# Two tiles per tanh in the last layer group of a fused attention and MLP kernel, with new scheduler priorities

## The chip, the cores and the metric

The kernel runs on one core of a Trainium2 chip. The metric is the device time of one execution in microseconds (us), the median of several runs. The profile is of one such execution.

## The reference

A sketched polynomial attention gives each of 4 x 1088 tokens a vector of 128 numbers (4 heads of 32), and an MLP without bias follows. Cut to what is computed:

```python
def phi(x):                       # S1, S2: 8 x 32
    a = einsum('rd,bhsd->bhsr', S1, x); b = einsum('rd,bhsd->bhsr', S2, x)
    return einsum('bhsi,bhsj->bhsij', a, b).reshape(..., 64)
kv = einsum('bhsf,bhsd->bhfd', phi(k), v);  z = sum(phi(k), axis=2)
x = einsum('bhsf,bhfd->bhsd', phi(q), kv) / (einsum('bhsf,bhf->bhs', phi(q), z)[..., None] + 1e-06)
x = x.transpose(0, 2, 1, 3).reshape(4352, 128)
h = x @ w_in                      # 128 x 2048
out = (h - tanh(h)) @ w_out       # 2048 x 128
```

q and k are drawn with a deviation of 0.5, v with 0.1. Inputs and the output are float32.

## The kernel before

The linear part h @ w_out is x @ (w_in @ w_out); the product of the two weights is formed once on the chip, as a high and a low bf16 part (`whi`, `wlo`). What is left is minus tanh(h) @ w_out, so the scalar engine (ACT) computes tanh with a scale of -1.

Two kinds of groups run over the tokens. Nine attention groups (`GROUPS`) of up to 20 blocks of 32 tokens go through these steps: `qT` transposes q, `p` projects it (L717, tiled f32 matmuls), `qq`, `au`, `dn`, `rd`, `an`, `qp` and `qpT` form products and denominators on the vector engine and GpSimd, `w` computes the numerators (L733, tiled f32 matmuls), and `x` casts the result to bf16 into `xT` (L812). The keys of each batch are handled by `kp` (L608, tiled f32 matmuls), `wk`, `gram`, `sums`, `turn`.

Eleven layer groups (`LAYERS` = 8, 14, 12, 14, 14, 14, 14, 12, 14, 12, 8 blocks of 32 tokens) do the MLP. In group g, for each of the 16 blocks jb of 128 hidden units:

- `h{g}_{jb}` (L898): one matmul of a 128 x 128 block of `w_in` with the group's tokens, into one of three PSUM banks that take turns (`h_bank`, banks 4 to 6);
- `t{g}_{jb}` (L902): one tanh on ACT from that bank into slot (16 g + jb) mod 40 of `tt`;
- `y{g}_{jb}` (L912): one matmul of a block of `w_out` with that slot, adding up in bank 7.

In group 0 (256 tokens) two blocks share a bank and a tanh (`two` is 2). The last two groups (9 with 384 tokens, 10 with 256) go through `last_rows`: tokens are the output's rows, so each `y{g}_{jb}_{y}` (L933) is a matmul of 128 tokens of a slot with a block of `w_out`, into a bank of its own for each 128 tokens y. `l{g}_{y}whi` and `l{g}_{y}wlo` add the linear part. Then a copy to SBUF (L942) and a store (L944) for each y; the last store is issued from ACT's queue.

The order of the work isn't written out. Every operation is put down with its engine, a cost, its dependencies and a priority (`P.op`). `Program.listed` plans in simulated time: it takes the engine that can start first, and of its operations that can start within 20 ns of that the one with the smallest priority number. On the tensor engine it prefers operations of the same kind (`mode`) as the last, and charges `MODE` = 92 ns for a change of kind. The planned order of each engine is then issued in order, with semaphores. An h or a t has priority 16 g + jb, a y that plus `LAG` = 12 (in `last_rows`, plus 10 + 0.1 y for group 9 and plus 12 + 8 y for group 10), and attention steps the priority of the layer group that needs them, less a few. `SHIFT` is a table of numbers added to the priorities of named operations:

```python
for tag, by in SHIFT.items():
    P.tags[tag].prio += by
```

The lines that the change touches are the table and these two at the head of the loop over hidden blocks:

```python
two = 1 if g else 2
for jb in range(0, NJB, two):
```

Of the kernel before, what the change touches and what calls it, by code (L numbers as in the profile page):

```python
# [15 lines left out]
NJB = DFF // 128  # L16
# [29 lines left out]
class Program:  # L46
# [210 lines left out]
    def emit(self):  # L257
# [64 lines left out]

SHIFT = {
# [21 lines left out]
}  # L345
TURNED = (0, 1, 3)

# [1 line left out]
def bass_polysketch_attn__then__act_tanh_shrink_kernel(nc, q, k, v, S1, S2, moe_w_in, moe_w_out, out):  # L349
    P = Program(nc)  # L350
# [4 lines left out]
    def pe(n):  # L355
        return n / 2.4 + 2.7

    def dve(n):
        return 100 + n / 0.96

    def act(n):
        return 52 + n / 1.2
# [53 lines left out]
    def h_bank():  # L416
        i = 4 + (n_hb[0] + 2) % NHB
        n_hb[0] += 1
        return ps[:, i, :], bank[i]
# [31 lines left out]
    NL = len(lays)  # L451
# [419 lines left out]
    def store(g):  # L871
        ob = out.rearrange("(b j c) e -> b j c e", b=B, j=32)
        o, u = 0, g % 2
        for b, c, nb in lays[g][0]:
            for cb in range(4):
                P.op("sync", 4096 * nb / 250, lambda e, b=b, c=c, nb=nb, cb=cb, o=o: e.dma_start(
                    out=ob[b, :, c:c + nb, 32 * cb:32 * cb + 32],
                    in_=osb[u][32 * cb:32 * cb + 32, 32 * o:32 * (o + nb)].rearrange("p (c x) -> p c x", x=32)),
                    r=[("osb", u)], sem=f"out{u}", prio=NJB * g)
            o += nb  # L880

    def layers(g):
        parts, nb, t0, of = lays[g]
        n = 32 * nb
        slot0 = NJB * g

        def lin(front):
            for x, nm in ((whi, "whi"), (wlo, "wlo")):
                P.op("tensor", pe(n), lambda e, x=x, f=front and x is whi, l=not front and x is wlo: e.matmul(  # L889
                    acc[:, 0:n], x[:, :], xT[:, t0:t0 + n], start=f, stop=l),  # L890
                    r=[(nm,)] + [("xT", x) for x in of], w=[ka], prio=slot0 + LAG + (0 if front else NJB))

        two = 1 if g else 2
        for jb in range(0, NJB, two):
            s = slot0 + jb
            bk, kb = h_bank()
            ts = s % TSLOTS
            P.op("tensor", two * pe(n), lambda e, jb=jb, bk=bk: [e.matmul(  # L898
                bk[:, n * x:n * x + n], w_in[:, 128 * (jb + x):128 * (jb + x) + 128], xT[:, t0:t0 + n], start=True, stop=True)
                for x in range(two)][-1],  # L900
                r=[("w_in", jb // 4)] + [("xT", x) for x in of], w=[kb], prio=s, tag=f"h{g}_{jb}")
            P.op("scalar", act(n * two), lambda e, ts=ts, bk=bk: e.activation(  # L902
                out=tt[:, ts:ts + two, 0:n], in_=bk[:, 0:n * two].rearrange("p (x n) -> p x n", x=two), func=AF.Tanh, scale=-1.0),
                r=[kb], w=[("t", ts + x) for x in range(two)], prio=s, tag=f"t{g}_{jb}")
        if g >= NL - ROWS:
            return last_rows(g)
        if g > 1:
            lin(True)
        for jb in range(NJB):
            s = slot0 + jb  # L910
            ts = s % TSLOTS
            P.op("tensor", pe(n), lambda e, jb=jb, ts=ts: e.matmul(  # L912
                acc[:, 0:n], w_out[:, jb, :], tt[:, ts, 0:n],
                start=(jb == 0 and g < 2), stop=(jb == NJB - 1 and g != 1)),
                r=[("w_out", jb // 4), ("t", ts)], w=[ka], prio=s + LAG, tag=f"y{g}_{jb}")
        if g == 1:
            lin(False)
        u = g % 2
        ob, ok = (osb[u], ("osb", u)) if g else (osx, ("osx",))
        P.op("vector", dve(n), lambda e: e.transpose(out=ob[:, 0:n], in_=acc[:, 0:n]),  # L920
             r=[ka], w=[ok], prio=slot0, tag=f"o{g}")
        if g:
            store(g)

    def last_rows(g):
        ((b, c, nb),), _, t0, of = lays[g]
        slot0 = NJB * g
        last = g == NL - 1
        o, banks, eng = (0, (2, 3), ("sync", "scalar")) if last else (2, (7, 0, 1), ("sync",) * 3)
        ob = out.rearrange("(b j c) e -> b j c e", b=B, j=32)  # L930
        for y in range(nb // 4):
            def rows(lhs, rhs, prio, r, first=False, last=False, y=y, tag=None):
                P.op("tensor", 56, lambda e: e.matmul(  # L933
                    ps[:, banks[y], 0:128], lhs, rhs, start=first, stop=last), r=r, w=[bank[banks[y]]], prio=prio, tag=tag)

            for x, nm in ((whi, "whi"), (wlo, "wlo")):
                rows(xT[:, t0 + 128 * y:t0 + 128 * y + 128], x[:, :], slot0 + (LAG if last else 10), [(nm,)] + [("xT", x) for x in of], nm == "whi", tag=f"l{g}_{y}" + nm)
            for jb in range(NJB):
                ts = (slot0 + jb) % TSLOTS
                rows(tt[:, ts, 128 * y:128 * y + 128], w_out[:, jb, :], slot0 + jb + (LAG + 8 * y if last else 10 + 0.1 * y),  # L940
                     [("w_out", jb // 4), ("t", ts)], False, jb == NJB - 1, tag=f"y{g}_{jb}_{y}")
            P.op("vector", dve(128), lambda e, y=y: e.tensor_copy(osl[:, o + y, :], ps[:, banks[y], 0:128]),  # L942
                 r=[bank[banks[y]]], w=[("osl", o + y)], prio=slot0, tag=f"o{g}_{y}")
            P.op(eng[y], 300, lambda e, y=y: e.dma_start(  # L944
                out=ob[b, :, c + 4 * y:c + 4 * y + 4, :], in_=osl[:, o + y, :]),
                r=[("osl", o + y)], sem=f"outl{o + y}", prio=slot0, mode="rows")
# [27 lines left out]
    for g in range(NG):  # L974
# [18 lines left out]
        if g == 1:  # L993
            layers(0)
        if g == 2:
            linear_turn(1, DUE_W - 3)
            linear_product(DUE_W)
            first_linear(DUE_W + 4)
            layers(1)
# [65 lines left out]
```

## Time and profile before

| | us |
|---|---|
| median of three runs | 102.39 (102.28 to 102.39) |
| the profiled execution | 102.28 |
| its span, from the first to the last profiled instruction | 100.5 |

| engine | busy us | instructions |
|---|---|---|
| PE, matmuls | 96.5 | 1231 |
| PEld, weight loads | 52.0 | 1231 |
| DVE, vector engine | 71.5 | 181 |
| ACT, scalar engine | 78.0 | 182 |
| POOL, GpSimd | 33.2 | 60 |

PE is the tensor engine's matmuls, PEld its weight loads, which overlap them. Matmuls are pipelined and their ends are modelled, so that a matmul's duration is longer than the time from its start to the next one's; the starts are what counts. In a group's line, the number after "|" is the busy time, then the mean ns of one, then the idle time before them and what ended it. In a line of the timeline or the chain the first number is the start, the second the duration in us, and "x4" says that four neighbours were merged. In the windows the columns are busy time and count of each engine, the granted clock, the share of the DMA engines and GB/s. L898 is line 898 of the kernel before.

### The profile page before, as it was taken

How to read it: one execution, taken by the hardware profiler on the slowest of the kernel's cores; microseconds unless marked ns; L12 is line 12 of the kernel's file. 1: busy time of each engine (PE TensorE's matmuls, PEld its weight loads, DVE VectorE, ACT ScalarE, POOL GpSimd, SP SyncE). 2: the span in 40 equal slices, each digit the busy share in tenths (PEclk: the TensorE clock that was granted, in tenths of full speed). 3: DMA queues.
4: the chain of work that ended last, by engine and by line, in shares of the span. 5: the costliest groups of instructions: out<-in, count | busy, mean ns of one | idle time of the engine just before them, and what ended most of it. 6: DMA issues, size and time to landing. Idle time of an engine off the chain costs nothing.

```text
span 100.5 us, 3032 instructions
## 1 busy us (share of the span) xinstructions
PE 96.5 (96%) x1231; PEld 52.0 (52%) x1231; DVE 71.5 (71%) x181; ACT 78.0 (78%) x182; POOL 33.2 (33%) x60
## 2 busy tenths in 40 slices
PE   6999999999999999999999999999999999999980
PEld 5446467544666444545544444455444444468970
DVE  3689977999869999978999999899577226002140
ACT  0005679998957849793899998898999999999960
POOL 5577388042842400596040029403018000000000
PEclk9999999999999999999999999999999999999998
DMA  2899978920389451310899032002201403100512
GB/s 77 284 281 236 382 237 290 325 66 4 71 285 231 121 91 26 52 33 0 258 273 231 5 49 42 7 0 39 45 14 22 69 0 60 25 0 12 98 42 75
DMA packets 22510, 11.21 MB, mean 112 GB/s; under 512 B 16096, under 2 KB 21216, under 8 KB 22496
## 3 DMA queue, kind: packets, MB, share of 16 engines
q1 hardware_dynamic: 18976, 7.44, 30.5%
q10 hardware_dynamic: 3520, 3.57, 11.5%
q8 instruction: 9, 0.15, 0.6%
q14 instruction: 5, 0.04, 0.1%
HBM read 8.78 MB, written 2.23 MB: 110 GB/s over the span
## 4 chain that ended last, share of the span: by engine, by line
PE 87%; DMA 5%; DVE 4%; ACT 2%; issue 1%; POOL 0%; POOLq 0%; DVEq 0%
PE ps L898 31%; PE ps L912 24%; PE ps L733 5%; PE ps L933 5%; PE ps L673 5%; PE ps L717 4%; PE ps L608 3%; PE ps L889 3%; DMA kraw<-in_k_dram 3%; ACT tt L902 2%; DMA out_dram<-osl 2%; DVE wk L634 1%; PE ps L547 1%; PE ps L849 1%; PE ps L645 1%; PE ps L684 1%
## 5 line engine op out<-in xcount | busy, mean ns | idle before, releaser
L902 ACT ACTIVATE tt<-ps 128x448 bf16<-128x448 f32 (+3 forms) x168 | 71.9, 544 | 6.5 <-PE ps L898 6.0
L898 PE MATMUL ps<-xT,w_in 128*128 128x448 bf16 (+2 forms) x176 | 50.7, 333 | 0.2
L912 PE MATMUL ps<-tt,w_out 128*128 128x448 bf16 (+2 forms) x144 | 39.3, 338 | 0.0
L898 PEld LDWEIGHTS ps<-xT,w_in 128*128 128x128 bf16 x176 | 16.2, 98 | 20.4 <-ACT tt L902 11.5
L634 POOL TENSOR_TENSOR wk<-kab 128x256 f32<-128x256 f32 (+1 forms) x18 | 12.2, 675 | 19.1 <-DVE kab L619 17.5
L792 POOL TENSOR_TENSOR qp<-an,qq 128x512 f32<-128x512 f32 (+5 forms) x12 | 12.4, 1033 | 18.4 <-DVE an L780 17.5
L912 PEld LDWEIGHTS ps<-tt,w_out 128*128 128x128 bf16 x144 | 14.1, 98 | 7.7 <-issue 0.5
L920 DVE STREAM_TRANSPOSE osb<-ps 128x448 f32<-128x448 f32 (+1 forms) x8 | 5.0, 627 | 11.4 <-PE ps L912 11.4
L799 DVE STREAM_TRANSPOSE qpT<-qp 128x448 f32<-128x448 f32 (+5 forms) x18 | 11.4, 658 | 0.3 <-POOL qp L792 0.2
L933 PE MATMUL ps<-w_out,tt 128*128 128x128 bf16 x80 | 8.1, 219 | 0.0
L681 ACT ACT_TABLE_LOAD x1 | 1.3, 1283 | 8.3 <-issue 8.3
L1035 POOL MEMSET mark<- 128x1 f32 x1 | 0.1, 99 | 22.3 <-DMA out_dram<-osl 22.3
L746 DVE STREAM_TRANSPOSE qq<-ps 128x448 f32<-128x448 f32 (+5 forms) x9 | 6.0, 671 | 1.7 <-PE ps L717 1.5
L547 PE MATMUL ps<-const-bfloat16-1.0 128*128 128x256 bf16 (+1 forms) x25 | 6.5, 394 | 0.8 <-PEq L1050 0.8
L812 DVE CAST xT<-ps 128x448 bf16<-128x448 f32 (+4 forms) x8 | 6.2, 773 | 1.5 <-PE ps L733 1.4
L933 PEld LDWEIGHTS ps<-w_out,tt 128*128 128x128 bf16 x80 | 6.4, 98 | 0.6
L601 DVE STREAM_TRANSPOSE kT<-kraw 128x576 f32<-128x576 f32 (+1 forms) x8 | 5.7, 730 | 1.0 <-DMA kraw<-in_k_dram 0.9
L695 DVE STREAM_TRANSPOSE qT<-qraw 128x448 f32<-128x448 f32 (+5 forms) x9 | 5.9, 654 | 0.2 <-DMA qraw<-in_q_dram 0.2
L733 PE MATMUL ps<-qpT,ndw 64*32 64x288 f32 (+5 forms) x144 | 5.7, 373 | 0.0
L717 PE MATMUL ps<-qT,wq 64*32 64x288 f32 (+5 forms) x144 | 5.7, 373 | 0.0
L634 DVE TENSOR_TENSOR wk<-kab,ps 128x512 f32<-128x512 f32 x8 | 5.4, 673 | 0.0
L673 PEld LDWEIGHTS ps<-wk,vx 128*32 128x32 f32 x288 | 4.3, 110 | 1.8 <-issue 1.6
(86 smaller groups left out, 89.0 us busy)
## 6 DMA issues: line engine op xcount, KB each, us to landing
kraw<-in_k_dram SPq DMA_DIRECT2D x3, 544.0 KB, 4.1
qraw<-in_q_dram SPq DMA_DIRECT2D x3, 544.0 KB, 6.0
vx<-in_v_dram SPq DMA_DIRECT2D x10, 144.0 KB, 4.2
out_dram<-osb SPq DMA_DIRECT2D x20, 56.0 KB, 1.9
w_in_f<-in_moe_w_in_dram ACTq DMA_DIRECT2D x2, 512.0 KB, 8.1
w_out_f<-in_moe_w_out_dram ACTq DMA_DIRECT2D x2, 512.0 KB, 8.9
vx<-in_v_dram SPq DMA_DIRECT2D x4, 112.0 KB, 5.6
out_dram<-osb SPq DMA_DIRECT2D x8, 48.0 KB, 1.9
```

Of the source, the lines that this page charges most:

```text
L547: P.op("tensor", 213 if x < 12 else 290, lambda e, n=1 if x < 16 else 2: e.matmul(ps[:, 3, 0:256 * n], ones[:, 0:128], ones[:, None, :].to ...
L634: P.op(eng, 60 + 64 * n if eng == "vector" else pool(64 * n), lambda e: e.tensor_tensor(out=wk[:, t0:t1, :, :].rearrange("p t h (i j) -> p ...
L673: ins = e.matmul(ps[32 * h:32 * h + 32, sbk, 0:64], vx[i][:, h, t, :], wk[:, t, h, :], start=(t == 0), stop=(t == 8), tile_position=(0, 32 ...
L717: ins = e.matmul(o, wq[64 * r:64 * r + 64, b, y, :, :].rearrange("p h x -> p (h x)"), src, start=True, stop=True, tile_position=(64 * r, 3 ...
L733: ins = e.matmul(ps[32 * h:32 * h + 32, 2 + u, 0:32 * nh], ndw[i][64 * u:64 * u + 64, 32 * h:32 * h + 32], src[64 * u:64 * u + 64, h // 2, ...
L792: P.op("vector" if dv else "gpsimd", 95 + 33.2 * m if dv else pool(32 * m), lambda e, lo=lo, dv=dv: e.tensor_tensor(out=qp[u][:, lo:lo + m ...
L799: P.op("vector", dve(32 * m), lambda e, lo=lo: e.transpose(out=qpT[u][:, 32 * lo:32 * (lo + m)], in_=qp[u][:, lo:lo + m, :].rearrange("p n ...
L812: P.op("scalar" if early else "vector", (act if early else dve)(32 * nb) - 35, lambda e: (e.copy if early else e.tensor_copy)(xT[:, x0:x0 ...
L898: P.op("tensor", two * pe(n), lambda e, jb=jb, bk=bk: [e.matmul(bk[:, n * x:n * x + n], w_in[:, 128 * (jb + x):128 * (jb + x) + 128], xT[: ...
L902: P.op("scalar", act(n * two), lambda e, ts=ts, bk=bk: e.activation(out=tt[:, ts:ts + two, 0:n], in_=bk[:, 0:n * two].rearrange("p (x n) - ...
L912: P.op("tensor", pe(n), lambda e, jb=jb, ts=ts: e.matmul(acc[:, 0:n], w_out[:, jb, :], tt[:, ts, 0:n], start=(jb == 0 and g < 2), stop=(jb ...
L933: P.op("tensor", 56, lambda e: e.matmul(ps[:, banks[y], 0:128], lhs, rhs, start=first, stop=last), r=r, w=[bank[banks[y]]], prio=prio, tag ...
```

## The change

The number of blocks per tanh becomes a list: 2 for all of group 0 as before, seven times 2 and then 1 and 1 for the last group, 1 elsewhere. The names `h10_1`, `h10_3` and so on up to `h10_13` no longer exist (a pair has its first block's name), and likewise for t. In `SHIFT` 3 entries go (`h10_5`, `h10_7`, `h10_13`), 23 get another number and 43 are new. The loop, and those entries that the text speaks of:

```diff
-        two = 1 if g else 2
-        for jb in range(0, NJB, two):
+        jb = 0
+        for two in [2] * 8 if g == 0 else [2] * 7 + [1, 1] if g == NL - 1 else [1] * NJB:
             s = slot0 + jb
             bk, kb = h_bank()
             ts = s % TSLOTS
-            P.op("tensor", two * pe(n), lambda e, jb=jb, bk=bk: [e.matmul(
+            P.op("tensor", two * pe(n), lambda e, jb=jb, bk=bk, two=two: [e.matmul(
...
-            P.op("scalar", act(n * two), lambda e, ts=ts, bk=bk: e.activation(
+            P.op("scalar", act(n * two), lambda e, ts=ts, bk=bk, two=two: e.activation(
...
+            jb += two
         if g >= NL - ROWS:
             return last_rows(g)
```

```
name      before   after
y1_9        15.0    26.1
turn2       92.7    54.2
p8           5.8    59.8
w8         128.0    77.7461
h10_5       -5.4       -
h10_7      -28.6       -
h10_13     -11.8       -
h5_14          -    34.2
w3             -   -34.1
kp2            -   267.2
h9_0           -    17.0
h10_6          -   -45.5
...
```

The other new numbers are of the same kinds: most belong to h and y operations of groups 1 to 10, a few to steps of the keys and of the attention groups.

44 rows, old and new, of the table SHIFT are left out of this document.

## The prediction

> **What bounds the kernel now.** I began with the page: the engine totals, the chain, and the costly groups.
>
> ```profile
> PE 96.5 (96%) x1231; PEld 52.0 (52%) x1231; DVE 71.5 (71%) x181; ACT 78.0 (78%) x182; POOL 33.2 (33%) x60
> ...
> PE 87%; DMA 5%; DVE 4%; ACT 2%; issue 1%; POOL 0%; POOLq 0%; DVEq 0%
> ...
> L902 ACT ACTIVATE tt<-ps 128x448 bf16<-128x448 f32 (+3 forms) x168 | 71.9, 544 | 6.5 <-PE ps L898 6.0
> ```
>
> The chain that ended last is matmuls for 87% of the span and ACT for 2%. TensorE's busy time is modelled, so 96% alone proves nothing; the chain and the start times must. ACT's 168 tanhs were kept idle 6.0 us by matmuls. So ACT is a second, nearly full engine behind TensorE. The change edits ACT's work in the last layer group (group 10, 256 tokens wide) and the order of work everywhere, so I asked which engine sets the pace in the last 15 us: the windows that part the span where group 10's first hidden matmul starts (92.08), and the chain from 82 us on.
>
> ```profile
> core 0: us, PE busy (x) PEld busy (x) DVE busy (x) ACT busy (x) POOL busy (x), PEclk, DMA share, GB/s
> 92.08:97.54 5.46, 5.46 (x82) 5.03 (x78) 0.88 (x4) 5.13 (x18) 0.00 (x0) 1.00 0.35 67
> 85.00:92.08 7.08, 7.08 (x60) 4.37 (x60) 0.65 (x1) 7.08 (x19) 0.00 (x0) 1.00 0.09 15
> ```
> ```profile
> by line: PE ps L898 41.5%; PE ps L933 31.2%; PE ps L912 20.4%; PE ps L733 4.5%; PE ps L889 2.4%; DVE osl L942 1.9%; issue 0.2%
> ...
> 84.78 0.19 PE ps L898
> 84.96 0.19 PE ps L912
> ...
> 92.36 0.28 PE ps L933 x5
> ...
> 96.72 0.80 PE ps L933 x14
> 97.54 0.29 DVE osl L942
> ```
>
> Both engines look full in both windows. The chain decides: from 82 us on it holds no ACT piece at all. Matmuls follow each other without a gap (448 columns at 84.78, the next at 84.96), the 128-column rows of L933 at 0.28 / 5 = 0.056 us each. After the last row come a copy and the output store. ACT is hidden behind TensorE, if barely.
>
> How much TensorE still loses in the last stretch I worked out by counting, from the windows of L933 and of L898 alone and from the timeline:
>
> ```profile
> 92.08:97.54 5.46, 5.46 (x66) 4.81 (x62) 1.00 0.35 67
> ```
> ```profile
> 92.08:97.54 5.46, 4.38 (x16) 1.52 (x16) 1.00 0.35 67
> ```
> ```profile
> 91.86 0.39 PE L933 MATMUL ps<-w_out,tt 128*128 128x128 bf16 x4
> ...
> 92.08 0.27 PE L898 MATMUL ps<-xT,w_in 128*128 128x256 bf16 x1
> ...
> 93.40 0.27 PE L898 MATMUL ps<-xT,w_in 128*128 128x256 bf16 x1
> ...
> 93.51 0.28 PE L933 MATMUL ps<-w_out,tt 128*128 128x128 bf16 x2
> ```
>
> Of the 66 rows of L933 four had started before 92.08 (the row at 91.86), so 62 are issued in the stretch, and 16 hidden matmuls. A hidden matmul holds the issue for 93.51 - 93.40 = 0.11 us. So 62 x 0.056 + 16 x 0.11 = 3.47 + 1.76 = 5.23 us of issue. The stretch runs from 92.08 to 96.72 + 0.80 = 97.52, which is 5.44 us. TensorE idles 5.44 - 5.23 = 0.21 us there, and no more.
>
> **The change part by part.**
>
> **The paired tanhs.** The change removes seven of group 10's sixteen tanhs: 14 tiles of 256 columns go into seven instructions of 512, the last two stay single. It removes no matmul: each pair's two hidden matmuls write the two halves of one bank. What ACT saves comes from two rows, the single form in the lines of the last stretch, and four queued tanhs of the 512 form (group 0's, already paired) in ACT's timeline:
>
> ```profile
> L902 ACT ACTIVATE tt<-ps 128x256 bf16<-128x256 f32 x16 | 4.6, 456 | 0.0
> ```
> ```profile
> 13.55 2.07 ACT L902 ACTIVATE tt<-ps 128x512 bf16<-128x512 f32 x4 [0.48 <-PE ps L898]
> ```
>
> Successive instructions overlap, so I take the pitch and not the duration. Singles: (4.6 - 0.456) / 15 = 0.276 us. Pairs: with the four lasting about 0.62 each, (2.07 - 0.62) / 3 = 0.483 us. A pair saves at most 2 x 0.276 - 0.483 = 0.069 us, seven save 0.48 us of ACT. But TensorE's work per tile, one hidden matmul and three rows, is 0.11 + 3 x 0.056 = 0.278 us, the same as the singles' pitch: TensorE can give ACT nothing faster. So the saving reaches the end only as far as it removes TensorE's idle 0.21 us. Bounds: 0 and 0.21. I take 0.2, because with two tiles per bank three banks hold six tiles rather than three, and a hidden matmul that waits for a bank is the only wait that I see in that stretch.
>
> The Trainium skill (ScalarE: Activation LUTs, What ACT_TABLE_LOAD costs) gives an ACTIVATE with immediates 186 ns + 0.833 N and an overlap of 93 ns, an estimated fixed 0.093 us per instruction, or 0.65 us for seven; the rows give 0.48, and neither gets past TensorE.
>
> **What the pairing adds.** A row that reads the first tile of a pair now waits for the longer tanh, 0.62 instead of 0.456 us, and for the second hidden matmul (0.11): 0.27 us later. What covers it is the rows left from group 9: of the 62, 32 belong to group 10 and 4 are its linear terms, so 26 are group 9's, worth 26 x 0.056 = 1.46 us. Cost nothing; without that cover 0.27 us once. The last two tiles stay single, so the end after the last tanh is as it was: rows, copies, stores. The last store starts from ACT's queue behind the tanhs, but waits for the last copy, so a shorter ACT does not bring it forward.
>
> **The priorities.** 66 operations get a new one. No instruction is added or removed; TensorE's order changes. What an order can win is where TensorE loses time now. Apart from the 0.21 us I see one repeated loss: a run of tiled f32 matmuls (L608, L717, L733, 16 instructions each) stops the issue before and after it. Two of these in a row pay once. From TensorE's timeline, two alone and a joined couple:
>
> ```profile
> 62.45 0.36 PE L898 MATMUL ps<-xT,w_in 128*128 128x448 bf16 x1
> 62.75 0.66 PE L733 MATMUL ps<-qpT,ndw 64*32 64x256 f32 x16
> 63.20 0.58 PE L717 MATMUL ps<-qT,wq 64*32 64x224 f32 x16
> 63.72 0.36 PE L898 MATMUL ps<-xT,w_in 128*128 128x448 bf16 x1
> ```
> ```profile
> 75.62 0.55 PE L898 MATMUL ps<-xT,w_in 128*128 128x384 bf16 x2
> 76.10 0.61 PE L733 MATMUL ps<-qpT,ndw 64*32 64x224 f32 x16
> 76.64 0.50 PE L898 MATMUL ps<-xT,w_in 128*128 128x384 bf16 x2
> ...
> 82.10 0.36 PE L898 MATMUL ps<-xT,w_in 128*128 128x448 bf16 x1
> 82.39 0.77 PE L733 MATMUL ps<-qpT,ndw 64*32 64x320 f32 x16
> 83.09 0.36 PE L898 MATMUL ps<-xT,w_in 128*128 128x448 bf16 x1
> ```
>
> Alone, 224 columns hold the issue 76.64 - 76.10 = 0.54 us and 320 columns 0.70, so 256 would hold it about 0.59 (a third of the way). Joined, 256 columns held it 0.45 and the following 224 columns 0.52. That saves 0.14 + 0.02. The second also doesn't pay the lead-in again: the hidden matmul at 82.10 held the issue 0.29 us instead of 0.19, so 0.10. A join is worth about 0.26 us. The planner charges 92 ns (MODE, line 27) for it, a third, so an order that it thinks better can break a join, or make one by the way. There are four such joins now, in the chain:
>
> ```profile
> 16.93 0.54 PE ps L733 x16
> 17.47 0.33 PE ps L717 x16
> ...
> 23.73 0.65 PE ps L608 x16
> 24.38 0.32 PE ps L733 x16
> ...
> 44.89 0.65 PE ps L717 x16
> 45.54 0.43 PE ps L733 x16
> ...
> 62.82 0.59 PE ps L733 x16
> 63.41 0.38 PE ps L717 x16
> ```
>
> The new shifts reach several runs that stand alone: w3 (-34.1) and kp2 (+267.2), turn2 (92.7 to 54.2) between p6 and w5, and p8 (5.8 to 59.8). From the diff alone I cannot see which pairs form or part. Bounds: two joins gained (-0.52 us) to two lost (+0.52). I take one gained, -0.26, by the runs named, which have more single neighbours to join than joins to lose.
>
> **p8 later** costs nothing within its slack. Its chain on VectorE and the hidden work that needs it:
>
> ```profile
> 77.70 0.83 DVE L799 STREAM_TRANSPOSE qpT<-qp 128x640 f32<-128x640 f32 x1
> ...
> 83.27 1.59 DVE L812 CAST xT<-ps 128x640 bf16<-128x640 f32 x1 [0.31 <-PE ps L733]
> ```
>
> The transpose ends at 78.53, and the numerators that read it start at 82.39: 3.9 us to spare. p8 and w8 also feed group 9's first hidden matmul, past the cast's end at 84.86.
>
> **Sum.** -0.2 and -0.26 are -0.46 us. The profiled execution took 102.28 us (span 100.5, and 1.78 around it), so 101.82; the median of the runs, 102.39, is 0.11 above, so 101.9.
>
> **The rivals.** A difference under about 0.2%, 0.2 us, can't be told from none here.
>
> *ACT is the bound in the last 15 us, and more comes.* For it: ACT is busy 7.08 of 7.08 us before 92.08. The Trainium skill (Perfetto Trace Analysis, Identifying the Most-Contended Engine) says that matmul busy time misleads and weight loads' share is to be read; by that TensorE had 38% free there (4.37 of 7.08). As a mechanism here: if TensorE had room before 92.08, rows of group 9 would move ahead of it; of the 26, the nine of the last three tiles can't, so 17 x 0.056 = 0.95 us, and ACT's own end, shortened by 0.48, would allow about half of it and earlier ACT idle time the rest. About 101.4. Against it: the chain's back-to-back starts; a 448-column matmul holds the issue 0.19 us whatever its weight load takes. So the trace doesn't bear the rule out where tiles are wide.
>
> *Nothing comes of it.* The pairs' 0.21 us stays (the waits for a bank move to the first pairs), and joins gained and lost cancel: 102.2 to 102.5.
>
> *Slower: joins are lost.* Place: the four couples above. Price 0.26 us each. It decides from the second on: one lost is eaten by the 0.2 us of the pairs, two leave 0.52 - 0.2 = +0.3 (102.7), three +0.6 (103.0). For it: the planner's price of a third, and new shifts on their neighbours (y1_9 behind the second couple, h5_14 ahead of the fourth). Against it: its rule at line 141 prefers to stay in the same kind of matmul.
>
> **How the numbers follow.** Forecast (one join, the tail's idle time): 0.42. More by ACT or by further joins: 0.18. Nothing: 0.15. Slower by lost joins: 0.25. Faster by over 0.2%: the first two, 0.60; within: 0.15; slower: 0.25. The range reaches from 101.3 (just past the ACT case) to 102.9 (two joins lost and the tail's 0.2 not won).
>
> **What would show it.** Right: seven 512-column tanhs at the end, ACT idle or waiting between them, TensorE's last stretch about 0.2 us shorter for the same 62 + 16 instructions, and five joins of f32 runs instead of four. Wrong: a last stretch shorter by over 0.4 us (rows moved ahead, so TensorE had room), fewer joins, new waits of hidden matmuls for a tanh after 92 us, or numerators of the last group after 86 us with ACT idle behind them.

## The result and the profile after

The changed kernel takes 102.98 us (median of 20 runs) against 102.50 us for the kernel before. The ratio is 1.005, with a 95% interval of 1.0032 to 1.0068: slower by 0.33 to 0.70 us. The forecast was 101.9.

Engine totals and chain of the changed kernel's page:

```profile
PE 97.2 (95%) x1231; PEld 52.3 (51%) x1231; DVE 71.3 (70%) x181; ACT 78.1 (77%) x175; POOL 33.2 (33%) x60
...
PE 88%; ACT 4%; DVE 3%; DMA 2%; issue 1%; POOL 0%; POOLq 0%
```

The work is the same, with seven instructions fewer on ACT, and TensorE still holds the chain. The profiled span grew by 1.4 us, from 100.5 to 101.9. Before dividing that up, one has to see how much of it belongs to the change. ACT's timeline shows the first cast to `xT`, whose operands are loads and the first attention group, in the changed kernel, in the kernel before, and in a second profile of the kernel before (the control below):

```profile
13.32 0.37 ACT L813 CAST xT<-ps 128x256 bf16<-128x256 f32 x1 [0.19 <-PE ps L739]
```
```profile
12.69 0.37 ACT L807 CAST xT<-ps 128x256 bf16<-128x256 f32 x1 [0.19 <-PE ps L733]
```
```profile
13.39 0.37 ACT L808 CAST xT<-ps 128x256 bf16<-128x256 f32 x1 [0.19 <-PE ps L734]
```

The same program differs by 0.70 us there from one execution to the next, so the start can't be compared between two profiles. In the changed kernel's execution another half microsecond went by ahead of group 1 (from this cast to group 1's first hidden matmul 6.06 us, against 5.57 before and 5.43 in the control). That isn't the change either: up to group 1's first hidden matmul the planned order of every engine is the same before and after, and the first experiment below, whose order differs from the changed kernel's by one later matmul, takes 5.36 us there. I count from the first hidden matmul of group 1, at 18.26 us before and at 19.38 after:

```profile
18.26 0.55 PE L898 MATMUL ps<-xT,w_in 128*128 128x448 bf16 x2
```
```profile
19.38 0.54 PE L904 MATMUL ps<-xT,w_in 128*128 128x448 bf16 x2
...
83.41 0.77 PE L739 MATMUL ps<-qpT,ndw 64*32 64x320 f32 x16
```

From there to the last numerators `w8` it is 82.39 - 18.26 = 64.13 us before and 83.41 - 19.38 = 64.03 after: the new priorities gained 0.1 us in the long middle. Behind `w8` the time is lost. This is TensorE's timeline there, VectorE's at the same place, and the waits from 84 to 88 us, all of the changed kernel:

```profile
84.88 0.35 PE L919 MATMUL ps<-tt,w_out 128*128 128x448 bf16 x1
85.06 0.54 PE L904 MATMUL ps<-xT,w_in 128*128 128x448 bf16 x2
85.92 0.23 PE L940 MATMUL ps<-whi,xT 128*128 128x128 bf16 x1 [0.31 <-DVE xT L818]
85.98 0.35 PE L919 MATMUL ps<-tt,w_out 128*128 128x448 bf16 x1
```
```profile
84.28 1.58 DVE L818 CAST xT<-ps 128x640 bf16<-128x640 f32 x1 [0.31 <-PE ps L739]
```
```profile
PEld ps L940 <- DVE xT L818: 0.7, 1, 0.7
...
PE ps L940 <- DVE xT L818: 0.3, 1, 0.3
```

Two hidden matmuls start at 85.06 and 85.25 (0.19 us apart) and should be followed at 85.44. The next matmul is `l10_0whi`, the first linear term of the last group. It reads what the last cast writes to `xT`, and it writes the bank that the cast reads. The cast ends at 85.86, and the matmul starts at 85.92. TensorE stands still for 85.92 - 85.44 = 0.48 us; the 0.31 in brackets counts only from the modelled end of the matmul before. The row behind it, at 85.98, needs nothing from the cast, but each engine takes its operations in the planned order. In the kernel before, `l10_0whi` stood 21 operations later, at 88.03, and found the cast done (84.86):

```profile
88.03 0.22 PE L933 MATMUL ps<-whi,xT 128*128 128x128 bf16 x1
```

The diff had put a shift of -8.1 on it.

The last stretch, from `w8` to the end of the last copy, shows what the rest of the change did. VectorE's last copies, before and after:

```profile
97.54 0.49 DVE L942 COPY osl<-ps 128x128 f32<-128x128 f32 x2 [0.99 <-PE ps L933]
```
```profile
98.73 0.68 DVE L949 COPY osl<-ps 128x128 f32<-128x128 f32 x2 [0.61 <-PE ps L940]
```

It took 98.03 - 82.39 = 15.64 us before and 99.41 - 83.41 = 16.00 after, 0.36 more. What the stretch would be without the standing still, the first experiment below shows: there `w8` starts at 82.60 and the last copies are

```profile
97.50 0.68 DVE L949 COPY osl<-ps 128x128 f32<-128x128 f32 x2 [0.61 <-PE ps L940]
```

That is 98.18 - 82.60 = 15.58 us. So the pairs and the new order of the last rows together are 0.06 us shorter, and of the 0.48 us of standing still 0.42 reach the end. The pairs themselves came out as they should, in the lines of ACT from 93.8 us on:

```profile
L908 ACT ACTIVATE tt<-ps 128x512 bf16<-128x512 f32 x7 | 3.6, 728 | 0.0
...
L908 ACT ACTIVATE tt<-ps 128x256 bf16<-128x256 f32 x2 | 0.8, 517 | 0.0
```

So aligned, the profile has -0.1 + 0.42 - 0.06 = +0.26 us up to the last copy. Behind it come 0.1 us more. From group 1's first hidden matmul to the end of the profiled execution it is 102.28 - 18.26 = 84.02 us before (102.86 - 18.82 = 84.04 in the control) and 103.77 - 19.38 = 84.39 after: +0.37 us, inside the interval of the runs (0.33 to 0.70).

### The profile page after: what moved, and what is told of

Its sections match the earlier page's. It is cut to its first block, busy times and chain, and to the rows that moved or that the text cites. A ratio compares the mean times of both kernels' runs of the same rounds, so it can differ in the third digit from the quotient of the medians.

```text
span 101.9 us, 3024 instructions
## 1 busy us (share of the span) xinstructions
PE 97.2 (95%) x1231; PEld 52.3 (51%) x1231; DVE 71.3 (70%) x181; ACT 78.1 (77%) x175; POOL 33.2 (33%) x60
## 4 chain that ended last, share of the span: by engine, by line
PE 88%; ACT 4%; DVE 3%; DMA 2%; issue 1%; POOL 0%; POOLq 0%
PE ps L904 29%; PE ps L919 23%; PE ps L940 5%; PE ps L553 5%; PE ps L739 5%; PE ps L679 5%; PE ps L723 4%; ACT tt L908 4%; PE ps L614 4%; PE ps L895 3%; DMA out_dram<-osl 2%; DVE xT L818 2%; PE ps L651 1%; DVE wk L640 1%; PE ps L855 1%
## 5 line engine op out<-in xcount | busy, mean ns | idle before, releaser
L904 PE MATMUL ps<-xT,w_in 128*128 128x448 bf16 (+2 forms) x176 | 48.8, 332 | 0.6 <-ACT tt L908 0.5
L919 PE MATMUL ps<-tt,w_out 128*128 128x448 bf16 (+2 forms) x144 | 38.8, 338 | 0.0
L904 PEld LDWEIGHTS ps<-xT,w_in 128*128 128x128 bf16 x176 | 15.3, 98 | 20.4 <-ACT tt L908 12.0
L940 PE MATMUL ps<-w_out,tt 128*128 128x128 bf16 x80 | 6.9, 219 | 0.0
L940 PEld LDWEIGHTS ps<-w_out,tt 128*128 128x128 bf16 x80 | 5.7, 98 | 0.7
L687 ACT COPY kvz<-ps 128x128 f32<-128x128 f32 x4 | 1.1, 266 | 5.9 <-PE ps L679 5.9
```

Source lines behind the costliest of these rows:

```text
L904: P.op("tensor", two * pe(n), lambda e, jb=jb, bk=bk, two=two: [e.matmul(bk[:, n * x:n * x + n], w_in[:, 128 * (jb + x):128 * (jb + x) + 1 ...
L919: P.op("tensor", pe(n), lambda e, jb=jb, ts=ts: e.matmul(acc[:, 0:n], w_out[:, jb, :], tt[:, ts, 0:n], start=(jb == 0 and g < 2), stop=(jb ...
L940: P.op("tensor", 56, lambda e: e.matmul(ps[:, banks[y], 0:128], lhs, rhs, start=first, stop=last), r=r, w=[bank[banks[y]]], prio=prio, tag ...
```

## The experiments

Theory A: the loss is this one wait. Theory B: it is the pairs or the other priorities, and the wait is made up later. Each result is a ratio to runs of the kernel before on the same chip.

**The shift taken out.**

```diff
-    "l10_0whi": -8.1,
```

> The changed kernel with one shift taken out, l10_0whi -8.1: the planner then puts that one matmul behind group 9's third hidden matmul again, and TensorE's order is otherwise the changed kernel's. Theory A (the loss is the 0.48 us for which TensorE stands still at this matmul until the last cast to xT has ended): that wait goes, about 0.5 us less than the changed kernel, so within 0.2 us of the kernel before. Theory B (the pairs or the other new priorities cost the time, the wait is made up later): stays about 0.4 to 0.5 us above the kernel before.

102.43 us against 102.42, ratio 0.9999 (0.9973 to 1.0025). The loss is gone. (The expectation has the place wrong: the matmul now stands behind group 9's first hidden matmul, not the third, and in the kernel before it stood behind the sixth.) TensorE's timeline in the same place has no gap; `l10_0whi` is now one of the two rows of L940 at 86.37, well behind the cast's end at 85.07:

```profile
84.83 0.35 PE L904 MATMUL ps<-xT,w_in 128*128 128x448 bf16 x1
85.02 0.54 PE L919 MATMUL ps<-tt,w_out 128*128 128x448 bf16 x2
85.40 0.35 PE L904 MATMUL ps<-xT,w_in 128*128 128x448 bf16 x1
...
86.37 0.27 PE L940 MATMUL ps<-whi,xT 128*128 128x128 bf16 x2
```

**The same matmul moved in the kernel before.**

```diff
+        pe, o = order["tensor"], self.tags["l10_0whi"]
+        pe.remove(o)
+        pe.insert(pe.index(self.tags["y8_1"]), o)
```

> The kernel before with one matmul moved in TensorE's planned order: l10_0whi stands ahead of y8_1, as in the changed kernel. Nothing else is moved. Theory A: the matmul waits for the cast, TensorE stands still about 0.45 us near 84.5 us of the span, and the time is 0.4 to 0.5 us above the kernel before. Theory B: no more than 0.1 us above it.

103.13 us against 102.42, ratio 1.0061 (1.0031 to 1.0092). One matmul of 0.056 us, moved, makes the kernel before as slow as the changed one, without a pair or a new priority. Its TensorE timeline:

```profile
84.58 0.35 PE L901 MATMUL ps<-xT,w_in 128*128 128x448 bf16 x1
85.24 0.23 PE L936 MATMUL ps<-whi,xT 128*128 128x128 bf16 x1 [0.32 <-DVE xT L815]
```

It was due at 84.58 + 0.19 = 84.77 and started at 85.24: 0.47 us.

**Two places later.**

```diff
+        pe.remove(self.tags["l10_0whi"])
+        pe.insert(pe.index(self.tags["h8_13"]) + 1, self.tags["l10_0whi"])
```

> The changed kernel with l10_0whi two matmuls later on TensorE (behind y8_1 and h8_13, 0.19 us each), all else in its place. Theory A: the matmul is reached 0.38 us later, so that of the 0.48 us of standing still 0.10 are left, and the time falls by about 0.4 us, to within 0.2 us of the kernel before. Theory B: stays about 0.5 us above it.

102.39 us against 102.56, ratio 0.9992 (0.9967 to 1.0016). The wait follows the place: from 0.48 to 85.01 - (84.71 + 0.19) = 0.11 us.

```profile
84.71 0.35 PE L907 MATMUL ps<-xT,w_in 128*128 128x448 bf16 x1
85.01 0.23 PE L943 MATMUL ps<-whi,xT 128*128 128x128 bf16 x1
```

**The operand earlier, the place kept.** The last cast becomes two, first the tokens of group 10 (`8b`), then those of group 9 (`8a`), and the two groups swap banks:

```diff
+        if g == NG - 1:
+            for nm, y0, y1 in (("8b", 3, 5), ("8a", 0, 3)):
+                P.op("vector", dve(128 * (y1 - y0)) - 35, lambda e, y0=y0, y1=y1: e.tensor_copy(
...
+        of = {9: ["8a"], 10: ["8b"]}.get(g, of)
...
-        o, banks, eng = (0, (2, 3), ("sync", "scalar")) if last else (2, (7, 0, 1), ("sync",) * 3)
+        o, banks, eng = (0, (0, 1), ("sync", "scalar")) if last else (2, (7, 2, 3), ("sync",) * 3)
```

> The changed kernel with TensorE's order as it is, l10_0whi at its early place too, but with its operand earlier: the last cast to xT is made as two, the 256 tokens of group 10 first (two fifths, about 0.64 us) and then the 384 of group 9, and groups 9 and 10 take each other's PSUM banks, so that the matmul needn't wait for the cast to have read its bank. Theory A: the matmul finds its operand 0.5 us before it is reached, no standing still there, 0.5 us less than the changed kernel. A theory by which the place of the matmul itself costs the time (it takes a slot from a hidden matmul, and ACT runs dry): stays 0.4 to 0.5 us above the kernel before.

102.44 us against 102.56, ratio 0.998 (0.9955 to 1.0006). TensorE's order is that of the changed kernel, and the wait is gone:

```profile
83.96 0.54 PE L912 MATMUL ps<-xT,w_in 128*128 128x448 bf16 x2
84.33 0.22 PE L949 MATMUL ps<-whi,xT 128*128 128x128 bf16 x1
84.39 0.35 PE L927 MATMUL ps<-tt,w_out 128*128 128x448 bf16 x1
```

So the early place itself costs nothing; only the unfinished cast does. Whether the matmul waited for what the cast writes or for the bank that it reads, no run separates: both are free when the cast ends. This is the lowest ratio of all, but its interval holds 1.

**Why the planner put it there.** It thinks that the last cast takes 100 + 640 / 0.96 - 35 = 732 ns (`dve`, `x_of`); the trace has 1.59 us. The cast of this group writes in a permuted order. With the right number the shift may stay:

```diff
-        P.op("scalar" if early else "vector", (act if early else dve)(32 * nb) - 35, lambda e: ...
+        P.op("scalar" if early else "vector", (act if early else dve)(32 * nb) - 35 if g < NG - 1 else 1590, lambda e: ...
```

> The changed kernel with one number of the planner set right: it is told 1590 ns for the last cast to xT (the profile's 1.59 us) instead of 732. With that, and with the shift of l10_0whi left in, the planner itself puts this matmul behind group 9's first hidden matmuls, where the cast has ended; all else is as in the changed kernel. Theory A (the wait for the cast, and its cause the planner's price): the 0.48 us go, within 0.2 us of the kernel before, as the kernel with the shift taken out. Theory B: 0.4 to 0.5 us above it.

The planner now puts `l10_0whi` just where it stands with the shift taken out; the order on every engine is the first experiment's. 102.65 us against 102.37, ratio 1.0017 (0.9998 to 1.0036). Two results for the same order, 0.9999 and 1.0017, also say how far apart two comparisons of one kernel can come.

**The control**, a second copy of the kernel before:

> The kernel before again, under another name and with a blank line more: how far two kernels with the same instructions come apart in such a comparison. All theories: the same, within 0.2 us. If it comes out 0.3 us off, the 0.3 to 0.4 us of the pairs alone and of the priorities alone are no more than such a spread.

102.52 against 102.37 us, ratio 1.0008 (0.9988 to 1.0029).

**The pairs alone and the priorities alone.** For the first, the loop's part of the diff on the kernel before; for the second, on the changed kernel:

```diff
-        for two in [2] * 8 if g == 0 else [2] * 7 + [1, 1] if g == NL - 1 else [1] * NJB:
+        for two in [2] * 8 if g == 0 else [1] * NJB:
...
-    "l10_0whi": -8.1,
```

> The kernel before with the paired tanhs alone: its own priorities, less the three whose names no longer exist. Theory A: no loss; between 0.2 us faster (TensorE's idle 0.21 us of the last stretch) and the same. Theory B with the pairs as the cause: 0.3 to 0.5 us slower.

> The changed kernel's priorities without l10_0whi's, and single tanhs in the last group. Theory A: within 0.2 us of the kernel before (TensorE's order up to 84 us gained 0.09 us in the profile of the changed kernel). Theory B with the priorities as the cause: 0.3 to 0.5 us slower.

Pairs alone: 102.79 us against 102.42, ratio 1.0037 (1.0016 to 1.0058). Priorities alone: 102.69 us, 1.0034 (1.0014 to 1.0054). Both miss theory A's range, though together they are the first experiment's kernel, which lost nothing. I ran the pairs again:

> The pairs alone again, as their 0.37 us over the kernel before have no place in the profile (TensorE's last stretch is as long as before, 15.00 us from the last numerators to the last matmul in both). If the pairs cost that time, 0.3 to 0.4 us above the kernel before again; if it was the spread of two comparisons, within 0.2 us of it.

102.85 us against 102.37, ratio 1.0049 (1.0023 to 1.0074): it repeats. Part of it the profiles show at the very end. In the pairs alone the last three stores are issued at 97.27, 97.92 (both SyncE) and 98.06 (ACT's queue); in the kernel before it was 96.66, 97.86 and 98.06, so the first of the three stood further off. The last one now lands after 2.1 us:

```profile
97.12 0.29 DVE L943 COPY osl<-ps 128x128 f32<-128x128 f32 x1 [0.18 <-PE ps L934]
97.73 0.29 DVE L943 COPY osl<-ps 128x128 f32<-128x128 f32 x1 [0.32 <-PE ps L934]
98.06 0.63 ACTq L945 DMA_DIRECT2D out_dram<-osl  x1
```
```profile
out_dram<-osl ACTq DMA_DIRECT2D x1, 64.0 KB, 2.1
```

In the kernel before it took 1.98 us, so 0.12 us are shown, in both profiles of the pairs alone. In the priorities alone the last two copies start at 97.78 and 97.98, behind a last single tanh that ends at 97.45. They end at 98.27 there, 15.83 us behind the start of `w8` (82.44), where it was 15.64 in the kernel before: 0.19 us later.

To test the order of the last rows I gave TensorE the first experiment's whole order behind `w8`, with the pairs in place and the old order ahead of it:

```diff
+        tail = [self.tags[x] for x in """...""".split()]
+        pe = order["tensor"]
...
+        pe[-len(tail):] = tail
```

> The pairs alone, with TensorE's order up to the last numerators as in the kernel before, and behind them as in the changed kernel without the shift of l10_0whi. If the 0.4 us of the pairs alone come from their order of the last rows (the last three stores bunched), the time is back within 0.2 us of the kernel before; if the pairs themselves cost it, it stays 0.3 to 0.5 us above.

102.55 us against 102.56, ratio 1.0005 (0.9985 to 1.0024). So the pairs cost about 0.4 us with the old order of the last rows, and nothing with the new one. The profiled executions, counted from group 1's first hidden matmul to the end, say much the same, with the second run of the pairs a little under its interval:

| kernel | execution, us | that matmul's start | the rest | over the kernel before | interval of the runs |
|---|---|---|---|---|---|
| before | 102.28 | 18.26 | 84.02 | | |
| control | 102.86 | 18.82 | 84.04 | +0.02 | -0.12 to 0.30 |
| changed | 103.77 | 19.38 | 84.39 | +0.37 | 0.33 to 0.70 |
| shift taken out | 102.53 | 18.55 | 83.98 | -0.04 | -0.28 to 0.26 |
| pairs alone | 102.53 | 18.29 | 84.24 | +0.22 | 0.16 to 0.59 |
| pairs alone, again | 102.76 | 18.55 | 84.21 | +0.19 | 0.24 to 0.76 |
| priorities alone | 102.63 | 18.40 | 84.23 | +0.21 | 0.14 to 0.55 |
| pairs, new last rows | 102.75 | 18.69 | 84.06 | +0.04 | -0.15 to 0.25 |

So the pairs with the old rows and the new rows with single tanhs each lose 0.2 us at the end, and the two together lose nothing: theory B is right of each half and wrong of the whole. The 0.2 of the priorities alone are the later copies (0.19) and 0.1 behind them, less the 0.1 gained in the long middle. Those of the pairs alone are the 0.12 of the last store (with the new rows it takes 1.98 us again) and 0.1 outside the profiled span: time less span averages 1.79 to 1.82 us in the kernels with single tanhs and 1.89 to 1.92 in all those with pairs, the changed one too. Why, no run shows. The other 0.2 that the runs give for the pairs alone I could not place.

**The price of a join**, the term on which the forecast rested:

```diff
+        pe.remove(self.tags["p7"])
+        pe.insert(pe.index(self.tags["h5_15"]) + 1, self.tags["p7"])
```

> The kernel before with p7 one hidden matmul later on TensorE, which parts one of the four couples of tiled f32 runs (w6 and p7). By the prediction's price 0.26 us slower; by the planner's 0.09.

102.68 us against 102.56, ratio 1.0011 (0.999 to 1.0031): the runs can't tell 0.26 from 0.09. The profile can. TensorE's timeline with the couple parted:

```profile
62.65 0.36 PE L901 MATMUL ps<-xT,w_in 128*128 128x448 bf16 x1
62.94 0.66 PE L736 MATMUL ps<-qpT,ndw 64*32 64x256 f32 x16
63.53 0.36 PE L901 MATMUL ps<-xT,w_in 128*128 128x448 bf16 x1
63.83 0.61 PE L720 MATMUL ps<-qT,wq 64*32 64x224 f32 x16
64.37 0.55 PE L915 MATMUL ps<-tt,w_out 128*128 128x448 bf16 x2
```

From the hidden matmul ahead to the matmul behind it takes 64.37 - 62.65 = 1.72 us, less the hidden matmul now in between (0.19): 1.53. Joined it was 63.72 - 62.45 = 1.27. The price is 0.26 us, as predicted.

**A join made on purpose**, on the first experiment's kernel:

```diff
+        pe.remove(self.tags["p6"])
+        pe.insert(pe.index(self.tags["w5"]), self.tags["p6"])
```

> The changed kernel without the shift of l10_0whi, and p6 moved in TensorE's planned order to stand right ahead of w5, so that two runs of tiled f32 matmuls that stood alone are joined. By the prediction's price of a join, 0.26 us faster than without the move, so 0.2 to 0.35 us faster than the kernel before, if VectorE's cast behind p6's chain (now about 1 us later) is still in time for layer group 5. If it isn't, hidden matmuls wait for it and the time is the same or up to 0.5 us longer.

103.11 us against 102.37, ratio 1.0072 (1.0046 to 1.0098): slower by 0.7 us. `p6` had stood behind `turn2`, an f32 matmul. Parted from it, `turn2` started at 51.28 and the hidden matmul behind it at 51.70, 0.42 us later; in the first experiment, with `p6` next, it held the issue 0.20 us (51.64 to 51.84). VectorE now waited a whole microsecond for `p6`, in the waits from 50 to 64 us:

```profile
DVE qq L755 <- PE ps L726: 1.0, 1, 1.0
```

From group 1's first hidden matmul to `w8` it took 83.14 - 18.17 = 64.97 us instead of 82.60 - 18.55 = 64.05. So the move made one join and undid another, and the order planned around the old place no longer fitted; how the 0.92 us divide between these was not taken apart. That a join made on purpose wins 0.26 us is not shown.

## Why the prediction was wrong, step by step

- **The priorities** are the step that failed. I bounded them by joins of f32 runs, from -0.52 to +0.52 us, and took one join gained. The price of a join was right (0.26 measured where one was parted); but the change makes none and parts none, the same four couples stand in its chain (at 17.96, 24.84, 46.01 and 63.88 us), so the -0.26 of the sum is 0. What the priorities did is not on my list, and no sign of being wrong that I named points at it: they put one matmul ahead of its operand, and TensorE stood still for 0.48 us, of which 0.42 reached the end.
- **p8 and the cast's end.** I looked for who needs the last cast, found group 9's first hidden matmul, and stopped. `l10_0whi` reads the same tile, stood in the diff with a new negative shift, and was not followed. The step needed one more sum from rows that I had quoted: the cast ends 2.47 us after `w8` starts (84.86 - 82.39), so any reader of its columns of `xT` that is issued less than that behind `w8` stands still. It also needed the right place of this matmul: I counted group 10's four linear rows among the 62 of the last stretch, where TensorE's timeline before has them from 88.03 to 88.20, four microseconds ahead of it. (The sum of 5.23 us goes by the count of 62 and stands; 30 rows are group 9's, not 26.)
- **The bound "tail, 0 to 0.21 us"** held for the whole last stretch: 0.06 us without the wait, where I took 0.2. That ACT's saving could not pass TensorE was right. Taking the end as untouched was wrong: with the old order of the rows, the last store takes 0.12 us longer behind the pairs, and every kernel with pairs spends 0.1 us more outside the span.
- **The slower rival** had the right sign and the wrong mechanism; its joins were not parted. What it said of the planner, that it misprices what it orders, was one part of the cause, on another price: 732 ns for a cast of 1.59 us. The other part is the shift of -8.1; with either one set right the wait is gone.
- **The ACT rival** fell. With the pairs the last stretch did not become shorter by more than TensorE's idle time.

## What to carry to other kernels

When priorities change in an engine that works in order, go through every operation that gets an earlier place, and ask of each when its operand and its output buffer are ready, not only of the operations at the centre of the change. A wrong price of the planner goes into every order that it makes: compare its costs with the trace for the slowest and the oddest forms before trusting an order that it finds better. And judge a bunch of small order changes by undoing one at a time: here a single one of 0.056 us of work was the whole loss. But halves of a change can lose where the whole does not: the pairs and the order of the last rows each cost 0.2 us without the other.

## What the runs showed of the hardware that was not expected

- VectorE's last cast takes 1.59 us for 640 columns, 2.5 ns each, where the other casts of 448 columns take 0.59 and 0.62 us, 1.3 to 1.4 ns each, and one of 576 takes 0.76 us. It is the one that writes bf16 in a permuted order; that the order is the reason is likely, but no run changed it alone.
- A stream of 128-column matmuls, each with its own weight load, starts every 0.056 us (14 in 0.80 us). The Trainium skill (TensorE: Matmul & The Clock Gate, Back-to-back issue gap) gives about 81 ns for such pairs and 56 ns for an isolated gap; the trace agrees with the second.
- The first 13 us differ by 0.7 us between two executions of the same program, so that profiles have to be aligned behind them.
